# Attention and two gated feed-forward blocks on one core: x summed in HBM by accumulating transfers, PSUM emptied by ScalarE, the last tokens written in place

## The chip, the cores and the metric

The kernel runs on one core of a Trainium2 chip: TensorE (PE in the rows), VectorE (DVE), ScalarE (ACT), GpSimd (POOL) and SyncE (SP), which here issues the transfers. The metric is the device time of one execution in microseconds, and lower is better.

## The reference

```python
# attention: B=8, H=8, S=576, D=64
q_s = softmax(q, over d); k_s = softmax(k, over s)
x = q_s @ (k_s^T @ v)                     # heads side by side: (8, 576, 512)
# first block
h = gelu_tanh(x @ w_in)                   # 512 -> 1024
u, v = halves of h
v_n = (v - mean) / sqrt(var + 1e-6) * g_ln
v_s = w_sg @ v_n + b_sg                   # over the 576 tokens
x = x + (u * v_s) @ w_out                 # 512 -> 512
# second block
h = relu(x @ w_in2)                       # 512 -> 1024
c = conv over tokens, width 3, one filter per channel
out = (h * sigmoid(c)) @ w_out2           # 1024 -> 512
```

All data are float32.

## The kernel before, in words

**Numbers.** TensorE reads float32r. A float32 operand is therefore split into a high part (rounded to float32r) and a low part (the rest), and a product is made of three matmuls: high by high, high by low, low by high. In the rows a trailing h or l names the part (gh, gl; yh, yl; xh, xl).

**The plan.** The program is first written down and then put in order. A class `Plan` records each instruction as a `Node` with its engine, its reads and writes; `price` gives each a cost and a latency by hand-set numbers, `deadlines` works backward from the end, and `order` is a list scheduler that puts out one queue per engine. All recorded instructions go out through one line, L403, so the line of a row tells nothing and the tiles' names do. Each engine works through its queue in order.

**Part one (to about 570 us).** For each of the 8 batches b the attention makes `x_hi[b]` and `x_lo[b]` (128 partitions x 4 chunks x 576 tokens). Softmax's scaling of q and k is done partly on GpSimd (`q<-q,qm`, `kt<-kt,scr`). Then the first block runs in 29 groups per batch, over two halves of 288 tokens. Of a half, `hv` and `hu` make v and u (gelu on ScalarE), `mx` applies w_sg, gl and gh are the parts of u times v_s, and `wo` multiplies by w_out into four PSUM tiles `acc`. When the fourth chunk is in (dc == 3), VectorE evacuates the four tiles, adding x_hi, into `x2s` (one buffer), and SyncE stores it to `x2d[b]` in HBM. x_lo goes to HBM by itself, as `xld[b]` (for batch 0 GpSimd adds it to x2s instead). While this runs, `split_far` splits the second block's weights into parts and stores them in HBM; the pieces in work are called wsl.

**Part two (from about 570 us).** Batches 0 and 1 are multiplied directly (`h2`). Batches 2 to 7 use seven products of half-size blocks in place of eight; GpSimd forms the sums of weights (`weight_sums`, tiles tk and tn) and of x (`operands`, tiles xf and xg). `load_x` loads x2d[b] as xf; `add_low` loads xld[b] in four pieces xg and GpSimd adds them. Per 128 channels the convolution runs on VectorE (a product and two three-operand steps `cv<-h,cw,cv`), ScalarE makes the sigmoid, and `gate` makes yh and yl, 576 tokens wide, for the product with w_out2 (`o2`, tiles wAh and wAl hold the weights). A batch's 576 tokens are four groups of 128 and one of 64. The last 64 tokens of an even batch and its odd neighbour are put side by side in `yL` by GpSimd (two casts per gate) and multiplied together (`o2_pair`).

Of the kernel before, what the change touches and what calls it, by code (L numbers as in the profile page):

```python
# [11 lines left out]
F32 = mybir.dt.float32  # L12
# [7 lines left out]
DM = H * D  # L20
# [4 lines left out]
MODES_ = 'dppddpddppdpdppdpdpddddp'  # L25
CFG = {'dord': 'qqkqqkqwkkwwv', 'start': 'kaaatabbktbkbqkTawtqbqtQvwwvxxqxswxlwLc', 'gh': 'aaa', 'x2': 'nnn', 'hvl': [6, 5, 3], 'qs': 'ppppd', 'qm': 'pppdp', 'vb': 2, 'gb': 2, 'kt': 'dddd', 'sgl': 'dppp', 'rh': 'pd', 'sw': 'ada', 'sl': 'ada', 'gl': 'ddd'}
GUARD = 1.125 * 2.0 ** -15

# [104 lines left out]
class Node:  # L133
    __slots__ = ("eng", "name", "args", "kw", "cost", "lat", "deps", "succ", "late", "unit", "shared", "table", "kb", "i", "left", "ready", "done", "t", "hook")

# [9 lines left out]
class Plan:  # L145
# [3 lines left out]
    def __init__(self, real):  # L149
        self.real, self.nodes, self.unit = real, [], 0  # L150
        for k in real:
            setattr(self, k, Engine(self, k))

    def begin(self):
        self.unit += 1

    def node(self, eng, name="", args=(), kw={}):
        n = Node()
        n.eng, n.name, n.args, n.kw, n.i, n.unit = eng, name, args, kw, len(self.nodes), self.unit
        n.deps, n.succ, n.table, n.kb, n.shared, n.cost, n.lat, n.hook = {}, [], None, 0, False, 0.0, 0.0, None  # L160
        self.nodes.append(n)
        return n

# [17 lines left out]
    def touch(self, n, v, write):  # L181
        b = v.tile
        if b.prev is not None:
            for m in b.prev.nodes:
                n.deps[m.i] = "start" if m.eng == n.eng != "sp" else "end"
        g = b.pool.gate
        if g is not None:
            n.deps[g.i] = "start"
        p, c = v.region()
        keep = []  # L190
        for e in b.log:
            m, ep, ec, ew = e
            if m is n:
                keep.append(e)
                continue
            hit = (ep & p) and (ec & c)
            if hit and (write or ew):
                n.deps[m.i] = "start" if m.eng == n.eng != "sp" else n.deps.get(m.i, "end")
            if not (write and (ep & ~p) == 0 and (ec & ~c) == 0):
                keep.append(e)  # L200
        keep.append((n, p, c, write))
        b.log = keep
        b.nodes.append(n)

    def price(self, n, out, ins):
# [18 lines left out]
        elif e == "act":  # L224
            n.cost = 0.15 + cols * 0.00091
            n.lat = n.cost + 0.12
            f = args_func(n)
            n.table = {"Gelu_apprx_tanh": "g", "Exp": "e", "Sigmoid": "s"}.get(f)
        elif e == "pool":
            if "tensor" in name:  # L230
                n.cost = 0.8 if cols == 1 else 0.2 + cols * (0.0008 if name == "tensor_copy" else 0.00195)
            else:
                n.cost = 0.05 + cols * 0.0009
            n.lat = n.cost + 0.1
            n.shared = True
        else:
            two = sum(v.tile.space != "psum" for v in ins) > 1 and not psum and name in ("tensor_tensor", "scalar_tensor_tensor")
            fast = not psum and name in ("tensor_scalar", "tensor_copy") and out.tile.dtype == F32
            n.cost = 0.07 + cols * (0.0066 if name == "reciprocal" else 0.00058 if fast else 0.00117)
            n.lat = n.cost + 0.07  # L240
            n.shared = (two or fast) and cols > 60

    def deadlines(self):
# [7 lines left out]
        for n in self.nodes:  # L251
            for d in n.deps:
                self.nodes[d].succ.append(n)
        for n in reversed(self.nodes):
            for s in n.succ:
                c = n.lat if s.deps[n.i] == "end" else 0.0
                n.late = min(n.late, s.late - c)

    def order(self):
# [41 lines left out]
        def start(n, t):  # L301
# [6 lines left out]
            if n.eng == "pool":  # L308
                if vecend[0] > t:
                    more = min(cost, vecend[0] - t) * 0.3  # L310
                    cost, lat = cost + more, lat + more
                poolend[0] = t + cost
# [99 lines left out]
def attn_gated_conv_kernel(ctx, tc, q, k, v, q0, k0, w_in, g_ln, w_sgT, b_sg, w_out, w_in2, conv_w, w_out2, out):  # L412
# [25 lines left out]
    x2d = [dram.tile([128, KC, S], F32, name=f"x2d{b}") for b in range(B)]  # L438
    xld = [dram.tile([128, KC, S], F32, name=f"xld{b}") for b in range(B)]
    w2d = [dram.tile([128, KC, FF2], F32, name=f"w2d{n}") for n in "hl"]  # L440
# [282 lines left out]
    def xt(b, hp):  # L723
# [101 lines left out]
    def wo(b, j):  # L825
# [160 lines left out]
    xt_left(0)  # L986
    xt_copy(0)
    def w_job(i):
        split(slots[ORDER[i]], *jobs[i], None)
# [52 lines left out]

    def split_far(src, d, k, n, behind):
        for c in range(k):
            for f in range(0, n, NW):
                fs = slice(f, f + NW)
                slot, h = parts[njob[0] % 2]
                njob[0] += 1
                split(slot, src[:, c, fs], far_h, slot[1].bitcast(F32R), NW, (pool, pool), [t[:, c, fs] for t in d], behind)

# [97 lines left out]
    for b in range(B):  # L1148
# [13 lines left out]
        for i, g in enumerate(groups):  # L1162
# [16 lines left out]
    wo2_hi, wo2_lo = w2["ohi"], w2["olo"]  # L1179
    yL = [p2.tile([128, NFC, 128], F32R, name=f"yL{n}") for n in "hl"]  # L1180
    later = []
    h_t = [w2["pool"].tile([128, S + 2], F32, name=f"h{i}") for i in range(3)]
# [36 lines left out]
    def gate(b, fc, h, cv):  # L1219
        yh = p2.tile([128, S], F32R, tag="yh", bufs=4)  # L1220
        yl = p2.tile([128, S], F32R, tag="yl", bufs=4)
        act.activation(cv, cv, AF.Sigmoid)
        dve.tensor_tensor(cv, cv, h[:, 1:S + 1], ALU.mult)
        act.activation(yh, cv, AF.Copy)
        dve.tensor_tensor(yl, cv, r32(yh), ALU.subtract)
        o = 64 * (b % 2)
        yL_hi, yL_lo = yL
        def copies():
# [3 lines left out]
        if any(o_[0] < b and b % 2 == 0 for o_ in oq):  # L1232
            later.append(copies)
        else:
            copies()
        y_t[b, fc] = (yh, yl)
# [24 lines left out]
    def o2_pair(b, fcs):  # L1261
# [4 lines left out]
        for fc in fcs:  # L1266
            mm3(lp["t"], yL_hi[:, fc], yL_lo[:, fc], wo2_hi[:, fc], wo2_lo[:, fc], fc == 0, fc == NFC - 1)
        if NFC - 1 in fcs:
# [10 lines left out]
    def do_o():  # L1279
        b_, fc_ = oq.pop(0)  # L1280
        o2(b_, fc_)
        if seen[b_] == NFC and b_ % 2 == 1 and b_ < B - 1:
            o2_pair(b_, range(NFC))
            while later:
                later.pop(0)()

    FIRST = 2
# [52 lines left out]
    def operands(b, xf):  # L1340
        q = {"11": xf[:, 0:2, 0:HALF], "12": xf[:, 2:4, 0:HALF], "21": xf[:, 0:2, HALF:S], "22": xf[:, 2:4, HALF:S]}
        s1 = p2.tile([128, S], F32, tag="xg", bufs=3).rearrange("p (c t) -> p c t", c=2)
        mine = opn[b] = {}
# [87 lines left out]
    for b in range(FIRST):  # L1431
        for fc in range(NFC):
# [10 lines left out]
            if b == 0 and fc >= 4:  # L1443
                add_low(1, xf, fc - 4)
# [84 lines left out]
```

## Time and profile before

| what | value |
|---|---|
| median of 3 runs | 981.03 us |
| lowest and highest | 979.24 and 983.11 us |
| profiled execution | 981.86 us |
| its span | 980.1 us |
| its mean granted TensorE clock | 0.988 |
| last matmul's end to the end of the span | about 7.3 us |

The span is what the profile's rows cover; the profiled execution is 1.8 us longer than it. A granted clock of 1.00 is TensorE's full speed. The busy time of an engine leaves out the issuing of transfers and waiting on semaphores.

### The profile page before, as it was taken

The page shows a single profiled execution, that of the slowest core. Times are in us where ns is not written, and L with a number is a line of the kernel's source. Part 1 is how long each engine was busy: PE and PEld are TensorE (multiplying, and loading weights), DVE is VectorE, ACT ScalarE, POOL GpSimd, SP SyncE. Part 2 cuts the span into 40 slices and gives each one's busy share as a digit, 9 for nine tenths or more (in the row PEclk, how much of TensorE's full clock was granted, in tenths as well). Part 3 has the DMA queues.
Part 4 walks back from the last instruction along what each step waited for, and adds up shares of the span by engine and source line. Part 5 has one row for each costly group of instructions (what it writes and reads, how often), then busy time and mean ns, then how long its engine had stood idle before and what let it go on. Part 6 is the DMA issues. An engine that isn't in the chain of part 4 may idle for free.

```text
span 980.1 us, 16191 instructions
## 1 busy us (share of the span) xinstructions
PE 934.7 (95%) x6026; PEld 825.9 (84%) x6026; DVE 784.5 (80%) x1391; ACT 556.9 (57%) x1063; POOL 458.2 (47%) x500
## 2 busy tenths in 40 slices
PE   5989989998999999999999998999999999999996
PEld 4567778987989889899999997888998889888985
DVE  6988989799788897976867379997888878887773
ACT  6878356845666458453634244444766566656662
POOL 5326363556353754554434079644354626362110
PEclk9999989999999999999999999999999999999999
DMA  9451534250352625534256631313121313121001
GB/s 294 139 171 66 148 121 133 104 170 17 127 175 91 178 65 167 148 108 141 85 191 202 226 133 45 107 35 106 46 96 45 106 46 105 36 82 33 18 27 54
DMA packets 55590, 107.42 MB, mean 110 GB/s; under 512 B 5716, under 2 KB 29268, under 8 KB 52824
## 3 DMA queue, kind: packets, MB, share of 16 engines
q1 hardware_dynamic: 55512, 106.39, 34.5%
q8 instruction: 47, 0.77, 0.3%
q14 instruction: 31, 0.25, 0.1%
HBM read 70.85 MB, written 35.53 MB: 109 GB/s over the span
## 4 chain that ended last, share of the span: by engine, by line
PE 60%; DVE 11%; POOL 3%; issue 3%; ACT 2%; DMA 1%; SPq 0%; DVEq 0%; ACTq 0%; POOLq 0%
PE mm L403 39%; PE acc L403 21%; DVE cv L403 4%; POOL tk L403 1%; DVE yl L403 1%; POOL xf L403 1%; DMA out<-ot 1%; DVE xl L403 1%; DVE wsl L403 1%; DVE scr L403 1%; DVE lt L403 0%; DVE h L403 0%; DVE gl L403 0%; ACT cv L403 0%; DVE ot L403 0%
## 5 line engine op out<-in xcount | busy, mean ns | idle before, releaser
L403 DVE SCALAR_TENSOR_TENSOR cv<-h,cw,cv 128x576 f32<-128x576 f32 x128 | 132.3, 1034 | 27.8 <-ACT cv L403 25.7
L403 POOL CAST yLh<-yh 128x64 fp32r<-128x64 f32 x64 | 38.6, 603 | 152.6 <-ACT yh L403 152.6
L403 PE MATMUL acc<-wAh,yl 128*128 128x512 f32 x256 | 102.8, 402 | 6.6 <-DVE yl L403 6.6
L403 PE MATMUL acc<-wAh,yh 128*128 128x512 f32 x256 | 102.8, 402 | 0.3 <-ACT yh L403 0.2
L403 PE MATMUL acc<-wAl,yh 128*128 128x512 f32 x256 | 102.3, 400 | 0.0
L403 PE MATMUL acc<-gl,wouth 128*128 128x288 f32 x256 | 78.5, 307 | 4.8 <-DVE gl L403 4.8
L403 PE MATMUL mm<-xh,w2h 128*128 128x288 f32 x280 | 82.6, 295 | 0.4 <-ACT ot L403 0.4
L403 PE MATMUL acc<-gh,wouth 128*128 128x288 f32 x256 | 82.9, 324 | 0.0
L403 PE MATMUL mm<-xl,w2h 128*128 128x288 f32 x280 | 82.5, 295 | 0.0
L403 PE MATMUL mm<-xh,w2l 128*128 128x288 f32 x280 | 82.3, 294 | 0.0
L403 PE MATMUL mm<-sgh,vnh 128*128 128x288 f32 x256 | 80.8, 315 | 0.0
L403 PE MATMUL mm<-xh,wAh 128*128 128x288 f32 x256 | 80.5, 315 | 0.1
L403 POOL TENSOR_TENSOR wsl<-wsl 128x256 f32<-128x256 f32 (+2 forms) x66 | 50.1, 761 | 59.8 <-ACT wsl L403 18.6
L403 PE MATMUL acc<-gh,woutl 128*128 128x288 f32 x256 | 77.9, 304 | 0.0
L403 PE MATMUL mm<-xh,wAl 128*128 128x288 f32 x256 | 75.7, 296 | 1.4 <-ACT wAl L403 1.4
L403 PE MATMUL mm<-sgh,vnl 128*128 128x288 f32 x256 | 75.5, 295 | 0.0
L403 PE MATMUL mm<-sgl,vnh 128*128 128x288 f32 x256 | 75.5, 295 | 0.0
L403 PE MATMUL mm<-xl,wAh 128*128 128x288 f32 x256 | 75.5, 295 | 0.0
L403 ACT ACTIVATE cv<-cv 128x576 f32<-128x576 f32 x64 | 43.7, 683 | 54.9 <-DVE cv L403 54.6
L403 POOL TENSOR_TENSOR q<-q,qm 128x512 f32<-128x512 f32 x56 | 61.6, 1129 | 20.5 <-DVE qm L403 13.4
L403 DVE TENSOR_TENSOR cv<-cv,h 128x576 f32<-128x576 f32 x64 | 59.2, 926 | 14.3 <-ACT cv L403 13.5
L403 PEld LDWEIGHTS acc<-wAh,yl 128*128 128x128 f32 x256 | 48.9, 191 | 20.7 <-DVE yl L403 8.8
(276 smaller groups left out, 3028.9 us busy)
## 6 DMA issues: line engine op xcount, KB each, us to landing
vt<-in_v SPq DMA_DIRECT2D x8, 1152.0 KB, 10.2
x2d<-x2s SPq DMA_DIRECT2D x16, 576.0 KB, 3.8
out<-ot SPq DMA_DIRECT2D x32, 256.0 KB, 2.0
kt<-in_k SPq DMA_DIRECT2D x7, 1152.0 KB, 5.7
xld<-xl SPq DMA_DIRECT2D x7, 1152.0 KB, 5.3
xf<-x2d SPq DMA_DIRECT2D x7, 1152.0 KB, 5.1
xg<-xld SPq DMA_DIRECT2D x28, 288.0 KB, 2.8
q<-in_q SPq DMA_DIRECT2D x28, 256.0 KB, 2.7
```

The lines of the kernel that those rows point to most:

```text
L403: getattr(self.real[n.eng], n.name)(*[val(a) for a in n.args], **{k: val(v) for k, v in n.kw.items()})
```

## The change

The change has four parts.

1. **x in HBM.** A new function `x_out(b)` stores x_hi to x2d[b] (SyncE) and then adds x_lo to it by a transfer that accumulates, issued by GpSimd. Each half of the w_out product is added to x2d in the same way. So xld, its loads as xg and GpSimd's adds of them are gone.
2. **Evacuation.** ScalarE copies the four acc tiles to x2s; VectorE did it before.
3. **Last tokens.** yh and yl are 512 tokens wide; ScalarE and VectorE write the last 64 straight into yL, which becomes a ring of 11 slots. GpSimd's casts and the list `later` are gone.
4. **The plan's numbers.** `price` has other costs for ScalarE, GpSimd and VectorE; a transfer issued by GpSimd costs 1.2 us and lands after 20. Of `split_far`'s 32 pieces one goes in per some four groups, by `soon` and FAR, where all were recorded at once; the weight sums are recorded at (0, 6) and (1, 2) and may not start before the matmul recorded last.

The number of transfers that GpSimd issues goes from 0 to 24 (8 of x_lo, 16 of x2s). SyncE loses 28 loads of xg, 7 stores to xld and 16 of x2s, and has 8 stores of x_hi more. The program of after has 29 table loads on ScalarE, that of before 45.

```diff
@@ price
         elif e == "act":
-            n.cost = 0.15 + cols * 0.00091
-            n.lat = n.cost + 0.12
+            n.cost = (0.155 if psum else 0.195) + cols * 0.00085
...
         elif e == "pool":
+            if "dma" in name:
+                n.cost, n.lat = 1.2, 20.0
+                return
...
@@ xt
-                sp.dma_start(xld[b], r32(x_lo[b]))
+                x_out(b)
...
+    def x_out(b):
+        sp.dma_start(x2d[b], r32(x_hi[b]))
+        pool.dma_start(x2d[b], r32(x_lo[b]), accum_op=ALU.add, max_dma_last_dim=2304)
@@ wo
             for m in range(4):
-                if CFG['x2'][min(b, 2)] == 'a':
-                    act.activation(x2s[:, m], acc["t"][m][:, 0:HALF], AF.Copy)
-                    pool.tensor_tensor(x2s[:, m], x2s[:, m], r32(x_hi[b][:, m, cs]), ALU.add)
-                else:
-                    dve.tensor_tensor(x2s[:, m], acc["t"][m][:, 0:HALF], r32(x_hi[b][:, m, cs]), ALU.add)
-                if b == 0:
-                    pool.tensor_tensor(x2s[:, m], x2s[:, m], r32(x_lo[b][:, m, cs]), ALU.add)
-            sp.dma_start(x2d[b][:, :, cs], x2s)
+                act.activation(x2s[:, m], acc["t"][m][:, 0:HALF], AF.Copy)
+            pool.dma_start(x2d[b][:, :, cs], x2s, accum_op=ALU.add)
...
-            if b == 1 and i == 0:
-                mark = next(n for n in reversed(plan.nodes) if n.eng == "pe")
-                split_far(w_in2_v, w2d, KC, FF2, mark)
-                split_far(w_out2_v, wo2d, NFC, DM, mark)
+            if far and 29 * b + i >= 37 + 140 * (32 - len(far)) / 32:
+                plan.soon(FAR, split_far)
...
@@ gate
-        yh = p2.tile([128, S], F32R, tag="yh", bufs=4)
-        yl = p2.tile([128, S], F32R, tag="yl", bufs=4)
+        yh = p2.tile([128, 512], F32R, tag="yh", bufs=YB)
+        yl = p2.tile([128, 512], F32R, tag="yl", bufs=YB)
         act.activation(cv, cv, AF.Sigmoid)
         dve.tensor_tensor(cv, cv, h[:, 1:S + 1], ALU.mult)
-        act.activation(yh, cv, AF.Copy)
-        dve.tensor_tensor(yl, cv, r32(yh), ALU.subtract)
...
-            pool.tensor_copy(yL_hi[:, fc, o:o + 64], r32(yh[:, 512:576]))
-            pool.tensor_copy(yL_lo[:, fc, o:o + 64], r32(yl[:, 512:576]))
...
+        act.activation(yh, cv[:, 0:512], AF.Copy)
+        dve.tensor_tensor(yl, cv[:, 0:512], r32(yh), ALU.subtract)
...
+        zh, zl = (t[:, sl, 64 * (b % 2):64 * (b % 2) + 64] for t in yL)
+        act.activation(zh, cv[:, 512:S], AF.Copy)
+        dve.tensor_tensor(zl, cv[:, 512:S], r32(zh), ALU.subtract)
...
-    def add_low(b, xf, c):
-        xg = p2.tile([128, S], F32, tag="xg", bufs=3)
-        sp.dma_start(xg, xld[b][:, c])
-        pool.tensor_tensor(xf[:, c], xf[:, c], xg, ALU.add)
...
@@ weight_sums
+        after = plan.last
...
-            pool.tensor_tensor(t, r32(wq[n][0][:, c]), r32(wq[n][1][:, c]), ALU.add)
+            pool.tensor_tensor(t, r32(wq[n][0][:, c]), r32(wq[n][1][:, c]), ALU.add).deps[after.i] = "start"
@@ operands, first()
-            for c in range(4):
-                add_low(b, xf, c)
             pool.tensor_tensor(s1, q["21"], q["22"], ALU.add)
@@ main loop of part two
-            if b == 1 and fc in (0, 2):
-                weight_sums(fc // 2)
+            if (b, fc) in SUMS:
+                weight_sums(SUMS.index((b, fc)))
```

**The order on GpSimd in part two.** Here one batch's operands begin, in the kernel before; xg holds a piece of the low part until it is the sum s1, and the numbers behind the names tell tiles apart.

```order
L403 TENSOR_TENSOR xf_5671<-xf_5671,xg_5721 128x576
L403 CAST yLh_5814<-yh_5964 128x64
L403 TENSOR_TENSOR xf_5671<-xf_5671,xg_5676 128x576
L403 CAST yLl_5842<-yl_5976 128x64
L403 TENSOR_TENSOR xf_5671<-xf_5671,xg_5715 128x576
L403 TENSOR_TENSOR xf_5671<-xf_5671,xg_5721 128x576
L403 TENSOR_TENSOR xg_5715<-xf_5671 128x576
L403 TENSOR_TENSOR xf_5671<-xf_5671 128x2x288
```

The four adds of the low part stand ahead of the batch's first sum, with casts of the gates between. The queue of after at one of the same places:

```order
L424 TENSOR_TENSOR xg_6043<-xf_5720 128x576
L424 TENSOR_TENSOR xf_5720<-xf_5720 128x2x288
L424 TENSOR_TENSOR xf_5720<-xg_6043,xf_5720 128x2x288
```

Only the sums of x are left there.

**The evacuation.** In the kernel before it stands in VectorE's queue; the words in brackets name the semaphores that an instruction waits for (DMAHW those of SyncE's transfers).

```order
L403 TENSOR_TENSOR xLl_100<-mm_138,xLh_97 128x4x64 [waits Activation_49]
L403 TENSOR_TENSOR x2s_131<-acc_0_205,xh_0_994 128x288 [waits DMAHW1_49,PE_49]
L403 TENSOR_TENSOR x2s_131<-acc_0_210,xh_0_994 128x288 [waits PE_49]
L403 TENSOR_TENSOR x2s_131<-acc_0_217,xh_0_994 128x288 [waits PE_49]
L403 TENSOR_TENSOR x2s_131<-acc_0_226,xh_0_994 128x288 [waits PE_49]
L403 STREAM_TRANSPOSE q_0_239<-q_0_239 128x512 [waits Pool_49]
```

After, it stands in ScalarE's queue, behind a gelu of v, and waits for a transfer that GpSimd issued (DMASW).

```order
L424 ACT_TABLE_LOAD
L424 ACTIVATE v_434<-mm_172 128x512 [waits PE_49]
L424 ACTIVATE x2s_130<-acc_0_205 128x288 [waits DMASW7_49]
L424 ACTIVATE x2s_130<-acc_0_210 128x288
L424 ACTIVATE x2s_130<-acc_0_219 128x288
L424 ACTIVATE v_411<-mm_181 128x512 [waits PE_49]
L424 ACTIVATE x2s_130<-acc_0_227 128x288
```

The work has moved to another engine, and what stands around it is the next batch's gelu in place of the attention's transposes.

**GpSimd in part one, after.** Where only the scaling of q and the splitting of weights stood, transfers now stand between; the second one here is of x_lo.

```order
L424 TENSOR_TENSOR q_0_212<-q_0_212,qm_721 128x512 [waits DMAHW3_49,DVE_49]
L424 DMA x2d_0_1614<-x2s_130 512x1x288 [waits DMASW5_49,Activation_49]
L424 TENSOR_TENSOR q_0_221<-q_0_221,qm_721 128x512 [waits DMAHW7_49]
...
L424 DMA x2d_0_2367<-xl_0_1044 128x4x576 [waits DMAHW5_49]
```

The transfer of a half waits for ScalarE and for an earlier accumulating transfer, and the next scaling of q stands behind it.

## Rows read from the trace of the kernel before

**Rows 1.** The profile's page: each engine's busy time, share of the span, instructions
```profile
PE 934.7 (95%) x6026; PEld 825.9 (84%) x6026; DVE 784.5 (80%) x1391; ACT 556.9 (57%) x1063; POOL 458.2 (47%) x500
```

**Rows 2.** Stretches: start:end, length, busy PE, PEld, DVE, ACT, POOL, clock, DMA, GB/s
```profile
20.00:100.00 80.00, 76.64 (x452) 54.04 (x452) 69.40 (x136) 64.05 (x123) 32.48 (x32) 1.00 0.44 136
100.00:240.00 140.00, 130.51 (x914) 116.34 (x913) 123.83 (x271) 79.00 (x147) 73.64 (x77) 0.95 0.41 121
...
560.00:640.00 80.00, 73.08 (x448) 65.75 (x447) 68.93 (x70) 33.41 (x62) 61.42 (x50) 0.98 0.32 107
720.00:740.00 20.00, 17.86 (x108) 16.08 (x107) 17.53 (x21) 11.69 (x23) 15.45 (x13) 1.00 0.28 90
820.00:840.00 20.00, 18.22 (x104) 16.21 (x103) 18.39 (x21) 12.80 (x26) 15.40 (x13) 0.92 0.33 103
```

**Rows 3.** The same view in steps of 10 us
```profile
120.00:130.00 10.00, 8.33 (x59) 7.62 (x57) 9.59 (x21) 1.49 (x3) 6.04 (x6) 1.00 0.70 225
130.00:140.00 10.00, 8.95 (x39) 8.06 (x41) 7.39 (x20) 6.18 (x7) 8.36 (x10) 0.66 0.17 59
```

**Rows 4.** TensorE's waits, 20 to 560 us: total, times, longest
```profile
PE acc L403 <- DVE gl L403: 4.0, 3, 2.7
```

**Rows 5.** TensorE's waits, 560 to 960 us
```profile
PE acc L403 <- DVE yl L403: 5.9, 4, 2.5
PE mm L403 <- DVE h L403: 3.9, 2, 2.1
```

**Rows 6.** VectorE's groups, 580 to 640 us: busy us, mean ns | idle before
```profile
L403 DVE SCALAR_TENSOR_TENSOR cv<-h,cw,cv 128x576 f32<-128x576 f32 x19 | 28.0, 1474 | 0.4
L403 DVE TENSOR_TENSOR cv<-cv,h 128x576 f32<-128x576 f32 x10 | 11.6, 1162 | 1.2 <-ACT cv L403 1.1
```

**Rows 7.** VectorE's groups, 920 to 960 us
```profile
L403 DVE SCALAR_TENSOR_TENSOR cv<-h,cw,cv 128x576 f32<-128x576 f32 x15 | 12.2, 821 | 6.8 <-ACT cv L403 6.5
...
L403 DVE TENSOR_TENSOR cv<-cv,h 128x576 f32<-128x576 f32 x7 | 5.2, 755 | 2.3 <-ACT cv L403 2.3
```

**Rows 8.** GpSimd's groups over the whole span
```profile
L403 POOL TENSOR_TENSOR xf<-xf,xg 128x576 f32<-128x576 f32 x28 | 46.0, 1656 | 2.6 <-DMA xf<-x2d 2.6
...
L403 POOL CAST yLh<-yh 128x64 fp32r<-128x64 f32 x64 | 38.6, 603 | 152.6 <-ACT yh L403 152.6
```

**Rows 9.** GpSimd's groups, 580 to 640 us
```profile
L403 POOL TENSOR_TENSOR xf<-xf,xg 128x576 f32<-128x576 f32 x8 | 14.1, 1767 | 0.0
...
L403 POOL CAST yLh<-yh 128x64 fp32r<-128x64 f32 x9 | 6.3, 696 | 8.1 <-ACT yh L403 8.1
L403 POOL CAST yLl<-yl 128x64 fp32r<-128x64 f32 x9 | 5.5, 610 | 2.2 <-DVE yl L403 2.2
```

**Rows 10.** Groups of ScalarE and VectorE over the whole span
```profile
L403 ACT ACT_TABLE_LOAD x45 | 57.7, 1283 | 3.1 <-PE mm L403 1.7 <-PEq L1519 0.7
...
L403 ACT ACTIVATE tk<-mm 128x288 f32<-128x288 f32 x72 | 28.4, 399 | 6.9 <-PE mm L403 6.8
...
L403 DVE TENSOR_TENSOR x2s<-acc,xh 128x288 f32<-128x288 f32 x64 | 26.2, 451 | 5.1 <-PE acc L403 3.6 <-DMA wsl<-in_w_out 1.5
```

**Rows 11.** Tile x2s: issues, ns min/median/max, first and last start
```profile
L403 SPq DMA_DIRECT2D x2d<-x2s x16: 524/560/2640, 119.3 to 570.4; - x16
```

**Rows 12.** The page's DMA issues: KB each, median us from issue to landing
```profile
vt<-in_v SPq DMA_DIRECT2D x8, 1152.0 KB, 10.2
x2d<-x2s SPq DMA_DIRECT2D x16, 576.0 KB, 3.8
```

**Rows 13.** Timeline of SyncE's queue: start, length, both in us
```profile
188.44 0.53 SPq L403 DMA_DIRECT2D x2d<-x2s  x1
...
556.32 0.56 SPq L403 DMA_DIRECT2D x2d<-x2s  x1
```

**Rows 14.** Timeline of VectorE at the next evacuations
```profile
207.32 1.54 DVE L403 TENSOR_TENSOR x2s<-acc,xh 128x288 f32<-128x288 f32 x4
...
568.69 1.66 DVE L403 TENSOR_TENSOR x2s<-acc,xh 128x288 f32<-128x288 f32 x4 [0.62 <-PE acc L403]
```

More of the change, by code (lines that the diff above doesn't have):

```diff
@@ L133 @@
 class Node:
-    __slots__ = ("eng", "name", "args", "kw", "cost", "lat", "deps", "succ", "late", "unit", "shared", "table", "kb", "i", "left", "ready", "done", "t", "hook")
+    __slots__ = ("eng", "name", "args", "kw", "cost", "lat", "deps", "succ", "late", "unit", "shared", "table", "kb", "i", "left", "ready", "done", "t", "hook", "due")
 class Engine:
@@ L149, in __init__, with soon @@
     def __init__(self, real):
-        self.real, self.nodes, self.unit = real, [], 0
+        self.real, self.nodes, self.unit, self.due, self.last = real, [], 0, None, None
         for k in real:
             setattr(self, k, Engine(self, k))
+    def soon(self, lead, job):
+        self.due = (self.last, lead)
+        job()
+        self.due = None
     def begin(self):
@@ L159, in node @@
         n.eng, n.name, n.args, n.kw, n.i, n.unit = eng, name, args, kw, len(self.nodes), self.unit
-        n.deps, n.succ, n.table, n.kb, n.shared, n.cost, n.lat, n.hook = {}, [], None, 0, False, 0.0, 0.0, None
+        n.deps, n.succ, n.table, n.kb, n.shared, n.cost, n.lat, n.hook, n.due = {}, [], None, 0, False, 0.0, 0.0, None, self.due
         self.nodes.append(n)
+        if eng == "pe":
+            self.last = n
         return n
@@ L184, in touch @@
             for m in b.prev.nodes:
-                n.deps[m.i] = "start" if m.eng == n.eng != "sp" else "end"
+                n.deps[m.i] = "start" if m.eng == n.eng and "dma" not in m.name else "end"
         g = b.pool.gate
@@ L197, in touch @@
             if hit and (write or ew):
-                n.deps[m.i] = "start" if m.eng == n.eng != "sp" else n.deps.get(m.i, "end")
+                n.deps[m.i] = "start" if m.eng == n.eng and "dma" not in m.name else n.deps.get(m.i, "end")
             if not (write and (ep & ~p) == 0 and (ec & ~c) == 0):
@@ L229, in price @@
         elif e == "pool":
+            if "dma" in name:
+                n.cost, n.lat = 1.2, 20.0
+                return
             if "tensor" in name:
-                n.cost = 0.8 if cols == 1 else 0.2 + cols * (0.0008 if name == "tensor_copy" else 0.00195)
+                wide = any(o[0] == "to_broadcast" for v in views for o in v.ops)
+                n.cost = 0.95 if cols == 1 else 0.2 + cols * (0.0008 if name == "tensor_copy" else 0.00164 if wide else 0.0021)
             else:
@@ L238, in price @@
             fast = not psum and name in ("tensor_scalar", "tensor_copy") and out.tile.dtype == F32
-            n.cost = 0.07 + cols * (0.0066 if name == "reciprocal" else 0.00058 if fast else 0.00117)
+            n.cost = 0.15 + cols * (0.0062 if name == "reciprocal" else 0.00055 if fast else 0.00104)
+            if len(ins) > 2 or (fast and len(ins) > 1):
+                n.cost += min(cols, 500) * 0.00013
             n.lat = n.cost + 0.07
@@ L254, in deadlines @@
         for n in reversed(self.nodes):
+            if n.due:
+                n.late = n.due[0].late + n.due[1]
             for s in n.succ:
@@ L309, in start @@
                 if vecend[0] > t:
-                    more = min(cost, vecend[0] - t) * 0.3
+                    more = min(0.5, vecend[0] - t)
                     cost, lat = cost + more, lat + more
@@ L987, in attn_gated_conv_kernel @@
     xt_copy(0)
+    x_out(0)
     def w_job(i):
@@ L1041, in attn_gated_conv_kernel, with split_far @@
     njob = [0]
[L1043 to L1049, printed above, removed]
+    far = []
+    for src, d, kc, n in ((w_in2_v, w2d, KC, FF2), (w_out2_v, wo2d, NFC, DM)):
+        far += [(src, d, c, slice(f, f + NW)) for c in range(kc) for f in range(0, n, NW)]
+    def split_far():
+        src, d, c, fs = far.pop(0)
+        slot, h = parts[njob[0] % 2]
+        njob[0] += 1
+        split(slot, src[:, c, fs], far_h, slot[1].bitcast(F32R), NW, (pool, pool), [t[:, c, fs] for t in d], plan.last)
     far_h = p1.tile([128, NW], F32R, name="farh")
@@ L1179, in attn_gated_conv_kernel, with last_slot @@
     wo2_hi, wo2_lo = w2["ohi"], w2["olo"]
-    yL = [p2.tile([128, NFC, 128], F32R, name=f"yL{n}") for n in "hl"]
-    later = []
+    NL = NFC + 3
+    yL = [p2.tile([128, NL, 128], F32R, name=f"yL{n}") for n in "hl"]
+    held = {}
+    def last_slot(b, fc):
+        turn_ = fc if b < FIRST else 2 * (fc % 4) + (fc < 4)
+        return (b // 2 * NFC + turn_) % NL
     h_t = [w2["pool"].tile([128, S + 2], F32, name=f"h{i}") for i in range(3)]
@@ L1219, in gate @@
     def gate(b, fc, h, cv):
-        yh = p2.tile([128, S], F32R, tag="yh", bufs=4)
-        yl = p2.tile([128, S], F32R, tag="yl", bufs=4)
+        yh = p2.tile([128, 512], F32R, tag="yh", bufs=YB)
+        yl = p2.tile([128, 512], F32R, tag="yl", bufs=YB)
         act.activation(cv, cv, AF.Sigmoid)
         dve.tensor_tensor(cv, cv, h[:, 1:S + 1], ALU.mult)
-        act.activation(yh, cv, AF.Copy)
-        dve.tensor_tensor(yl, cv, r32(yh), ALU.subtract)
-        o = 64 * (b % 2)
-        yL_hi, yL_lo = yL
-        def copies():
-            pool.tensor_copy(yL_hi[:, fc, o:o + 64], r32(yh[:, 512:576]))
-            pool.tensor_copy(yL_lo[:, fc, o:o + 64], r32(yl[:, 512:576]))
[L1232 to L1235, printed above, removed]
+        act.activation(yh, cv[:, 0:512], AF.Copy)
+        dve.tensor_tensor(yl, cv[:, 0:512], r32(yh), ALU.subtract)
+        sl = last_slot(b, fc)
+        assert held.get(sl, (b // 2, fc)) == (b // 2, fc)
+        held[sl] = (b // 2, fc)
+        zh, zl = (t[:, sl, 64 * (b % 2):64 * (b % 2) + 64] for t in yL)
+        act.activation(zh, cv[:, 512:S], AF.Copy)
+        dve.tensor_tensor(zl, cv[:, 512:S], r32(zh), ALU.subtract)
         y_t[b, fc] = (yh, yl)
@@ L1283, in do_o @@
             o2_pair(b_, range(NFC))
-            while later:
-                later.pop(0)()
-    FIRST = 2
     xg2 = {}
```

15 lines of the change are left out of this document (11 added, 4 removed).

## The prediction

> **What bounds the kernel now.** I read the busy times first: TensorE is busy 934.7 us, 95% of the span [rows 1]. The change leaves all matmuls as they are, only in another order, so it can recover only what TensorE loses: idle time, and time at a lower granted clock. The table by stage says where that is [rows 2]. 20 to 100 us: 80 − 76.64 = 3.4 us idle. 100 to 240: 140 − 130.51 = 9.5 idle, at a granted clock of 0.95, which costs another 0.05 × 140 = 7.0. 560 to 640: 6.9 idle and 0.02 × 80 = 1.6 of clock. 720 to 740: 2.1 idle. 820 to 840: 1.8 idle and 0.08 × 20 = 1.6 of clock. The clock comes from the idle time: TensorE stands 1.7 us of the ten from 120, and in the ten from 130 the granted clock is 0.66 with TensorE busy 8.95 [rows 3]; part of that stretch ran at 1.2 instead of 2.4 GHz. Sum: 19.9 us in part one (3.4 + 9.5 + 7.0) and 14.0 in part two (8.5 + 2.1 + 3.4): 33.9 in all. I leave the first 20 us and the tail out, since their work stays.
>
> Next, for whom TensorE waits there. In part one its longest wait is for VectorE's gl, 4.0 us in three waits [rows 4]; in part two for VectorE's yl, 5.9 in four, and its h, 3.9 in two [rows 5]. VectorE is busy 123.83 of 140 us in the first of these stretches and 17.53 and 18.39 of 20 in the last two [rows 2]: it, not ScalarE (79.00 of 140) or GpSimd, is late. Why it is late in part two can be seen where the same instruction is held against itself: the convolution's three-operand step takes 1474 ns from 580 to 640, and the add of the gate 1162 [rows 6]; from 920 to 960, where GpSimd has little left to do, 821 and 755 [rows 7]. VectorE is slowed by work of GpSimd beside it.
>
> **The change, part by part.** *GpSimd's adds and casts go.* Over the whole run: 46.0 us of 28 adds of the low part of x, and 38.6 of 64 small casts [rows 8], beside 64 more of the same size. From 580 to 640 they are 14.1 + 6.3 + 5.5 = 25.9 us [rows 9], 42% of the 61.42 that GpSimd is busy from 560 to 640 [rows 2]; the sums of weights and operands stay. Were GpSimd silent there, VectorE would save 19 × (1474 − 821) + 10 × (1162 − 755) ns = 12.4 + 4.1 = 16.5 us. 42% of that is 7, about the 6.9 idle there. The two later stretches hold the same adds and casts, GpSimd busy 15.45 and 15.40 of 20 [rows 2].
>
> *The last 64 tokens* cost VectorE a subtract of 64 columns more per gate, against 64 columns less in the one before. No row has the small one: no more than the 451 ns of a 288-column evacuation [rows 10], no less than what the shorter one saves (64/576 of about 1 us, 0.1). For nine gates between 580 and 640 that is −0 to +3.2 us net; I take +1, nearer to the low end, since 64 columns are far fewer than 288. ScalarE gets a copy in the same manner, and is busy 33.41 of 80 there [rows 2]: hidden. So part two gives back 7 − 1 = 6 of 6.9 in its first stretch; with the clock and the two others in the same proportion, I take 12 of the 14.0.
>
> *The evacuation of the w_out product* goes from VectorE to ScalarE: VectorE loses 64 × 451 ns = 26.2 us, ScalarE gains about 64 × 399 = 25.5, by the row of its copies of 288 columns, and loses 16 of its 45 table loads of 1283 ns, 20.5 us [rows 10]. It stays under 60% busy, so this is hidden, unless ScalarE waits (below). 1.64 us of VectorE in each of 16 halves; 140 us hold four of them, 6.6 us, so VectorE would go from 123.83 to about 117 in the stretch where TensorE stands 9.5 us. But VectorE still has its bursts, and the rest of the attention's operations stay; no row says which burst is shortened. Bounds: nothing, or all 19.9. I take 4 of the 9.5, half of the clock (3.5), and 0.5 of the 3.4: 8.
>
> *The order* comes from new planner costs. What it gains or loses by itself can't be read from a row; outside the stretches of the sum I count no loss of TensorE, so a worse order can only lose there. I take 0, with ±6 us (a third of part one's 19.9) in the range.
>
> *24 accumulating transfers issued by GpSimd.* None is in the trace before. Issue: SyncE spends 560 ns in the median and 2640 at most on such a store [rows 11]; 24 of them make 13 to 63 us on GpSimd, which is idle 66 of the 140 us from 100 [rows 2], and is otherwise relieved by the adds and casts of part two. Behind them in GpSimd's queue stand the key and query products that attention needs; 0.56 to 2.64 us late each, hidden as long as GpSimd is ahead. But the issue of a half also waits, by its order, for ScalarE's evacuation and for the transfer that wrote the same rows of x2d before, and holds GpSimd's queue meanwhile; a queue held for as long as the landing, 10 us, would show in VectorE and TensorE. Landing: no shorter than the plain store of these 576 KB, 3.8 us; I take twice a 1152 KB load, 2 × 10.2 = 20 us, as the upper bound, since an accumulation reads and writes [rows 12]. Middle: 10. What waits for it: x2s has one buffer, so the next half's evacuation, now on ScalarE, waits for the landing, and v's and u's gelus stand behind it in ScalarE's queue. Once in a batch that window is narrow: the stores of a half at 188.4 and 556.3 us [rows 13] are followed by the next evacuation at 207.3 and 568.7 [rows 14], 18.9 and 12.4 us later. The new order puts the evacuation behind one more gelu of v, so a landing of 12 to 20 us fits in. At 10 nothing waits.
>
> The Trainium skill speaks against this part: by "SBUF — State Buffer", section "SBUF: two separate sides", a transfer issued from GpSimd has its descriptors written by GpSimd's cores, and while VectorE runs in a mode that takes both of its ports, GpSimd is locked out and the descriptors starve. No run here yet shows an issue from GpSimd; that VectorE and GpSimd hold each other up is what [rows 6, 7] show. By that rule the transfers would be late just where VectorE is busiest, which is the fourth rival.
>
> *Loads.* 28 reloads of low parts and 7 stores of them go from SyncE, and 8 stores of x come; nothing in TensorE's waits is for a transfer there, so 0.
>
> **The sum.** The profiled execution spans 980.1 us and took 981.86; the median of the runs is 981.03. 981.86 − 8 − 12 = 961.9, and 0.8 less by the median: **961 us**.
>
> **The rivals.**
> 1. *Forecast* (chance 0.55): both parts give some, 953 to 970.
> 2. *Everything goes* (0.10): VectorE has enough slack that no stall and no dip of the clock is left: 981 − 33.9 = 947. For it: VectorE is the only one waited for at length. Against it: it is still busy over 80% from 100 to 240 then, and a burst needs no average.
> 3. *Only part two* (0.13): the new order and GpSimd's issues cost part one what VectorE gains there: 981 − 12 = 969 or so, up to 974. For it: part one's waits are short and for several tiles, so no one of them is removed by name.
> 4. *The wait changes its place* (slower, 0.12): the accumulation lands later than the window, some 18 us. From there each of the 8 batches loses the excess once in ScalarE's queue, with gelus and then matmuls behind it. At 27 us of landing that is 8 × 9 = 72 us, less the 20 gained: about 1030; at 22 us, 8 × 4 − 20 = 12: 993. For it: one buffer, and a queue in which the wait blocks everything behind it. Against it: 576 KB land in 3.8 us when stored plainly.
> 5. *No change* (0.10): GpSimd's adds did not slow VectorE, but the weight sums did, which stay, or GpSimd's 24 issues of 2 to 3 us each give back what is gained: 976 to 986. For it: from 580 to 640, 58% of GpSimd's work remains.
>
> **The numbers.** I hold a change of less than 0.5% (4.9 us) for no change that a measurement of this kernel could tell. Faster: rivals 1 to 3, 0.55 + 0.10 + 0.13 = 0.78. Same: 0.10. Slower: 0.12. The range takes in "everything goes" at its lower end and reaches into "no change" at its upper: 946 to 979; outside lie the slower case and half of the fifth.
>
> **What would show it.** Right: from 560 to 640, idle time of TensorE falls from 6.9 to 2 us or less, and the three-operand step takes nearer 1200 than 1474 ns; the granted clock of 100 to 240 rises above 0.95; VectorE is busy some 7 us less there. Wrong: ScalarE waits for the queue of GpSimd's transfers ahead of x2s with TensorE waiting for v or u behind it (rival 4), GpSimd's issues stand before key or query products for which TensorE waits (rivals 3 and 5), or the three-operand step keeps its 1474 ns with the adds gone (rival 5). The forecast falls as a whole if TensorE's idle time from 20 to 240 us grows above the 12.9 (3.4 + 9.5) that it is now.

## The result, and the profile after

The changed kernel takes 966.18 us in the median of 4 runs (965.54 to 969.03), the kernel before 981.26 in the same comparison (979.24 to 983.11, 4 runs): a ratio of 0.9852, 95% interval 0.9825 to 0.988. The forecast was 961, between 946 and 979. The profiled execution took 965.54 us, 3.6 more than the 961.9 that the sum gave for it.

The same stretches as in [rows 2], of after (columns as there):

```profile
20.00:100.00 80.00, 77.32 (x475) 55.20 (x474) 65.66 (x131) 61.16 (x118) 34.63 (x32) 1.00 0.57 168
100.00:240.00 140.00, 132.50 (x936) 118.71 (x935) 119.09 (x254) 74.23 (x153) 70.61 (x71) 0.98 0.56 136
...
560.00:640.00 80.00, 76.30 (x469) 69.41 (x469) 63.12 (x82) 36.47 (x80) 30.15 (x21) 0.98 0.19 58
...
720.00:740.00 20.00, 20.00 (x122) 18.11 (x121) 17.33 (x31) 14.82 (x33) 1.45 (x1) 1.00 0.14 54
...
820.00:840.00 20.00, 20.00 (x121) 18.08 (x120) 15.87 (x27) 13.46 (x28) 1.44 (x1) 1.00 0.08 32
```

From 720 to 740 and from 820 to 840 TensorE no longer stands, and the granted clock of the second is 1.00 in place of 0.92. From 560 to 640 it stands 3.7 us in place of 6.9, at the same 0.98. From 100 to 240 it stands 7.5 in place of 9.5, at 0.98 in place of 0.95. The DMA engines are busier from 20 to 240 (0.57 and 0.56 in place of 0.44 and 0.41). Of the signs that the prediction set, the granted clock and the three-operand step (below) came; the idle time from 560 to 640 stayed above the 2 us named, and VectorE lost 4.7 us from 100 to 240 in place of some 7.

TensorE's waits of after, 20 to 560 us and behind the dots 560 to 960, as in [rows 4, 5]:

```profile
PE mm L424 <- DVE kvd L424: 5.1, 3, 3.7
...
PE acc L424 <- DVE gl L424: 0.8, 2, 0.5
...
PE acc L424 <- DVE yl L424: 3.4, 2, 2.0
```

The wait for gl has shrunk from 4.0 to 0.8, that for h is gone, and a wait for kvd is now the longest in part one. VectorE's groups from 580 to 640 us, as in [rows 6]:

```profile
L424 DVE SCALAR_TENSOR_TENSOR cv<-h,cw,cv 128x576 f32<-128x576 f32 x20 | 19.4, 972 | 0.4
L424 DVE TENSOR_TENSOR cv<-cv,h 128x576 f32<-128x576 f32 x11 | 12.3, 1118 | 2.0 <-ACT cv L424 2.0
L424 DVE TENSOR_TENSOR yl<-cv,yh 128x512 fp32r<-128x512 f32 x11 | 10.5, 955 | 2.2 <-ACT yh L424 2.1
...
L424 DVE TENSOR_TENSOR yLl<-cv,yLh 128x64 fp32r<-128x64 f32 x11 | 5.7, 516 | 0.0
```

The three-operand step takes 972 ns in place of 1474. The new subtract of 64 columns takes 516 in the mean, though it has an eighth of the columns of yl's (955). Its row from 920 to 956 us, where GpSimd does nothing in this trace:

```profile
L424 DVE TENSOR_TENSOR yLl<-cv,yLh 128x64 fp32r<-128x64 f32 x7 | 1.5, 220 | 0.3 <-ACT yLh L424 0.3
```

The 516 is a mean of two lengths. Of the 64 small subtracts in the whole trace, 55 take 210 to 225 ns. The other 9 take 1309 to 1471; each of them starts while GpSimd is at a tensor-tensor instruction and ends some 80 ns behind that one's end. One of them, from the timelines of GpSimd and of VectorE (start, length in us):

```profile
607.45 1.80 POOL L424 TENSOR_TENSOR tn0l<-tk,tn0h 128x512 fp32r<-128x512 f32 x1
608.03 1.31 DVE L424 TENSOR_TENSOR yLl<-cv,yLh 128x64 fp32r<-128x64 f32 x1
```

The three-operand steps of the kernel before tell GpSimd's two kinds of work apart. Counted in the records of its trace, 59 of the 128 overlap nothing on GpSimd by more than 0.1 us and take 817 ns in the mean, 34 overlap casts alone and take 813, and 35 overlap a tensor-tensor instruction and take 1614. So it is the adds and sums on GpSimd that hold VectorE up here, and not the casts. In the changed kernel 13 of the 128 overlap a tensor-tensor instruction.

The accumulating transfers, first the page's DMA issues (KB each, us to landing), with SyncE's plain store of x_hi:

```profile
x2d<-xh SPq DMA_DIRECT2D x8, 1152.0 KB, 5.0
x2d<-xl POOLq DMA_DIRECT2D x8, 1152.0 KB, 13.1
x2d<-x2s POOLq DMA_DIRECT2D x16, 576.0 KB, 6.9
```

and the rows of tile x2s (ns min/median/max):

```profile
L424 ACT ACTIVATE x2s<-acc x64: 391/412/454, 108.4 to 571.1; 128x288 f32<-128x288 f32 x64
...
L424 POOL DMA_DIRECT2D x2d<-x2s x16: 1204/1231/1242, 110.4 to 572.0; - x16
```

An accumulation of a half lands in 6.9 us where the plain store of [rows 12] took 3.8, that of x_lo in 13.1 where the plain store of x_hi, as large, takes 5.0. Issuing one of a half takes GpSimd 1.2 us. The next evacuation follows no sooner than 19.6 us behind an issue in this trace, so ScalarE never waits for a landing: its waits ahead of x2s are for TensorE alone.

Where the longest wait for kvd comes from, 3.7 of the 5.1 us, shows in the chain of after between 188 and 201 us (start, length, what):

```profile
188.19 9.16 DMA wsl<-in_w_in
...
197.44 0.10 ACT wsl L424
...
198.42 0.44 ACT gh L424
...
199.97 0.28 DVE kvd L424
200.27 0.30 DVE kvd L424
...
200.62 0.43 PE mm L424 x2
```

and in GpSimd's timeline just before it:

```profile
183.03 1.24 POOL L424 DMA_DIRECT2D x2d<-x2s  x1 [1.49 <-ACT x2s L424]
183.74 1.85 POOL L424 DMA_DIRECT2D x2d<-xl  x1
```

The load of a far weight piece, wsl, is issued at 188.19 and takes 9.16 us, while the accumulation of x_lo issued at 183.74 is in flight (it lands at 197.7). ScalarE waits for the piece; the making of gh stands behind it in ScalarE's queue; VectorE waits for gh, with kvd behind it; TensorE waits for kvd. Over the whole of part one (140 to 570 us), the far pieces' loads and stores, counted one by one in the records of the traces:

```
              no accumulation in flight    one in flight
kernel        count  mean us  max us       count  mean us  max us
before           70     3.13     5.7           0
after            24     2.47     5.1          46     4.81     9.3
```

The longer time beside an accumulation shows in each of the six kinds of far transfer by itself. It is not the mark of an accumulation alone: in two kernels below that have none, e1 and e4, a far store of 128 KB took 9.6 and 8.4 us at the longest, each issued 0.7 us behind a 1152 KB load of v.

### The profile page after: what moved, and what is told of

Its sections match the earlier page's. It is cut to its first block, busy times and chain, and to the rows that moved or that the text cites. A ratio compares the mean times of both kernels' runs of the same rounds, so it can differ in the third digit from the quotient of the medians.

```text
span 963.8 us, 16047 instructions
## 1 busy us (share of the span) xinstructions
PE 927.9 (96%) x6026; PEld 822.1 (85%) x6026; DVE 751.7 (78%) x1391; ACT 558.5 (58%) x1175; POOL 361.4 (37%) x360
## 4 chain that ended last, share of the span: by engine, by line
PE 79%; DVE 12%; DMA 4%; ACT 3%; issue 2%; SPq 0%; POOL 0%; ACTq 0%; DVEq 0%
PE mm L424 53%; PE acc L424 25%; DMA wsl<-in_w_in 1%; DVE cv L424 1%; DVE qm L424 1%; DMA kt<-in_k 1%; DVE wsl L424 1%; DVE scr L424 1%; DVE xl L424 1%; ACT L424 1%; DVE gl L424 1%; DMA w2dh<-farh 1%; DVE vnl L424 1%; DVE lx L424 1%; DMA sgh<-in_q 1%
## 5 line engine op out<-in xcount | busy, mean ns | idle before, releaser
L424 DVE SCALAR_TENSOR_TENSOR cv<-h,cw,cv 128x576 f32<-128x576 f32 x128 | 113.5, 888 | 22.2 <-ACT cv L424 20.6
L424 POOL TENSOR_TENSOR q<-q,qm 128x512 f32<-128x512 f32 x56 | 63.9, 1202 | 28.9 <-DVE qm L424 12.9
L424 DVE TENSOR_TENSOR cv<-cv,h 128x576 f32<-128x576 f32 x64 | 56.9, 892 | 15.2 <-ACT cv L424 14.9
L424 POOL TENSOR_TENSOR kt<-kt,scr 128x512 f32<-128x512 f32 (+1 forms) x42 | 48.9, 1191 | 50.8 <-PE mm L424 37.2
L424 POOL TENSOR_TENSOR wsl<-wsl 128x256 f32<-128x256 f32 (+1 forms) x66 | 51.1, 775 | 43.5 <-DVE wsl L424 15.6
## 6 DMA issues: line engine op xcount, KB each, us to landing
x2d<-xl POOLq DMA_DIRECT2D x8, 1152.0 KB, 13.1
```

Source lines behind the costliest of these rows:

```text
L424: getattr(self.real[n.eng], n.name)(*[val(a) for a in n.args], **{k: val(v) for k, v in n.kw.items()})
```

## The experiments

Theory A, that of the prediction: the gain is work taken from GpSimd (part two) and from VectorE (part one). Rival P: the gain is the new order (the plan). After the first four runs a third was formed, theory C: accumulating transfers make the far pieces late, and the new order bears that better than the old.

For every kernel, TensorE's loss in part one (20 to 560 us) and in part two (560 to 840 us) was worked out as in the prediction, idle time plus (1 − granted clock) × length, from the stretches 20:100, 100:240, 240:400, 400:560, 560:640, 640:720, 720:740, 740:820, 820:840; the last but one column is what TensorE waited for kvd in part one, by the table of waits. Each loss is of one profiled execution, and the clock is read to two places, which can move a loss by about 1 us.

| kernel | median us | ratio to before, 95% | loss 1 | loss 2 | kvd us | what it has of the change |
|---|---|---|---|---|---|---|
| before | 981 | | 21.8 | 14.2 | 3.2 | nothing |
| after | 966.2 | 0.9852 (0.9825–0.988) | 15.8 | 5.4 | 5.1 | all |
| e1 | 977.7 | 0.9982 (0.9964–1.0001) | 20.0 | 7.4 | 1.0 | plan without VectorE's costs |
| e2 | 998.3 | 1.0193 (1.0166–1.022) | 33.7 | 16.5 | 10.6 | x, tokens |
| e3 | 967.4 | 0.9868 (0.9836–0.99) | 18.2 | 1.8 | 4.5 | plan, x |
| e4 | 967.4 | 0.9879 (0.9849–0.9909) | 10.0 | 10.0 | 0.3 | plan, tokens |
| e5 | 992.6 | 1.0111 (1.0075–1.0147) | 36.9 | 12.1 | 10.9 | x |
| e6 | 980.2 | 1.0002 (0.998–1.0025) | 17.7 | 15.1 | 3.2 | tokens |
| e7 | 996.6 | 1.0162 (1.0126–1.0198) | 41.6 | 7.2 | 15.6 | all but the costs |
| e8 | 976.8 | 0.9962 (0.9942–0.9982) | 20.8 | 12.0 | 8.2 | all but the spread |
| e9 | 960.0 | 0.9796 (0.9772–0.982) | 11.0 | 5.3 | 0.4 | all, far pieces later |
| e10 | 964.2 | 0.9842 (0.982–0.9864) | 13.4 | 2.1 | 0.7 | plan, tokens, 8 accumulations |
| e11 | 986.0 | 1.0055 (1.0037–1.0072) | 31.0 | 8.7 | 5.0 | e7 without x_lo |
| e12 | 965.1 | 0.9852 (0.981–0.9894) | 19.6 | 1.6 | none | e9 and e10 |

In e2, e5, e7 and e11 part one lasts 18 to 28 us longer (the last evacuation starts at 588 to 598 us, not at 570), so that the column of part two holds its end.

**e1, the plan alone, but for VectorE's costs.** On the kernel before, the new costs of ScalarE and GpSimd, `soon` and the spread of `split_far`, SUMS; nothing else. VectorE's costs, which the changed kernel has too, stay the old ones here, so that e1 is not the whole plan of which its expectation speaks.

```diff
-            if b == 1 and fc in (0, 2):
-                weight_sums(fc // 2)
+            if (b, fc) in SUMS:
+                weight_sums(SUMS.index((b, fc)))
```

> The kernel before with only the planner's new numbers (costs, spread of the far weight pieces, time of the weight sums); x by stores and reloads, evacuation on VectorE and GpSimd's adds and casts as before. Theory A, that the gain comes from work taken from GpSimd and VectorE: within 6 us of the time before, 975 to 987, and the three-operand step stays above 1300 ns from 580 to 640. Rival P, that the new order alone makes the gain: 971 or less.

977.71 us: theory A's range. The three-operand step keeps its length, since the adds beside it are still there:

```profile
L420 DVE SCALAR_TENSOR_TENSOR cv<-h,cw,cv 128x576 f32<-128x576 f32 x19 | 27.3, 1435 | 0.4
```

Yet the loss in part two fell from 14.2 to 7.4 with the same work. This much of the plan does little for the time, and it does do something for part two; what the whole plan does alone no run tells.

**e2, all but the plan.** The changed kernel with the old costs of ScalarE, GpSimd and VectorE (an accumulation keeps its price), with

```diff
-SUMS = ((0, 6), (1, 2))
+SUMS = ((1, 0), (1, 2))
...
-            if far and 29 * b + i >= 37 + 140 * (32 - len(far)) / 32:
-                plan.soon(FAR, split_far)
+            if b == 1 and i == 0:
+                mark = plan.last
+                while far:
+                    split_far(mark)
```

and without the weight sums' bound.

> The changed kernel with the planner's old costs, the far pieces recorded at once and the weight sums at (1, 0) and (1, 2); the work itself is that of the changed kernel. Theory A: the gain stays, 962 to 972. Rival P: it goes, 977 or more.

998.25 us: theory A falls as a sole cause, since the work without the plan is slower than the kernel before. P stands: it expected 977 or more, and e1, which gained nothing clear, lacks a part of the plan. Its chain ahead of a wait for kvd:

```profile
317.30 2.50 POOL x2d L419 x2
319.79 1.33 POOL wsl L419 x2
...
322.36 8.18 DMA w2dl<-wsl
...
331.56 0.29 DVE kvd L419
```

Two accumulations are issued at 317.3, the store of a far piece at 322.4 takes 8.18 us, and VectorE holds its queue for the piece's slot, with kvd behind. This is where theory C comes from.

**e3 and e4, one part of the work undone.** e3 gives the casts back to GpSimd:

```diff
-        act.activation(zh, cv[:, 512:S], AF.Copy)
-        dve.tensor_tensor(zl, cv[:, 512:S], r32(zh), ALU.subtract)
+        pool.tensor_copy(zh, r32(yh[:, 512:576]))
+        pool.tensor_copy(zl, r32(yl[:, 512:576]))
```

> The changed kernel with yh and yl 576 wide again and GpSimd's 128 casts into the ring of slots, in place of the copy on ScalarE and the subtract on VectorE. Theory A: GpSimd has 11.8 of its 25.9 us of 580 to 640 again and slows VectorE; 3 to 5 us slower than the changed kernel, about 970. Rival T, that the small subtracts on VectorE (516 ns each from 580 to 640) cost as much as the casts did: within 2 us of the changed kernel.

e4 gives x back its stores, reloads and adds, and VectorE its evacuation:

```diff
-                act.activation(x2s[:, m], acc["t"][m][:, 0:HALF], AF.Copy)
-            pool.dma_start(x2d[b][:, :, cs], x2s, accum_op=ALU.add)
+                dve.tensor_tensor(x2s[:, m], acc["t"][m][:, 0:HALF], r32(x_hi[b][:, m, cs]), ALU.add)
+            sp.dma_start(x2d[b][:, :, cs], x2s)
...
+            for c in range(4):
+                add_low(b, xf, c)
```

> The changed kernel with x as before: x_lo stored apart and reloaded, added by GpSimd, the w_out product evacuated by VectorE with x_hi added, no accumulating transfer. Theory A: VectorE has its 26 us of evacuations and GpSimd its 46 us of adds again; 7 us in part one and 4 to 6 in part two, 975 to 980. Rival P: within 3 us of the changed kernel, 963 to 969.

Both took 967.4. e3 bears out rival T: the casts cost no more than the subtracts, and TensorE has no idle time at all from 560 to 640 with the casts there, though the three-operand step takes 1225 ns in the mean from 580 to 640 (part one ends 5 us later here than in after):

```profile
560.00:640.00 80.00, 80.00 (x512) 74.09 (x511) 62.27 (x73) 36.25 (x71) 42.53 (x39) 1.00 0.26 74
```

e4 is out of theory A's range by 8 us, and within that of rival P. Its part one, with VectorE's 26 us of evacuations back, loses 10.0 us where after loses 15.8:

```profile
100.00:240.00 140.00, 134.39 (x997) 120.15 (x996) 127.71 (x281) 75.19 (x144) 71.95 (x75) 1.00 0.41 124
```

VectorE is busier there (127.71 against 119.09), and TensorE stands less (5.6 against 7.5) at full clock. Its part two, with the adds back, loses 10.0 where after loses 5.4, and the three-operand step takes 1191 ns where after's takes 972:

```profile
L424 DVE SCALAR_TENSOR_TENSOR cv<-h,cw,cv 128x576 f32<-128x576 f32 x18 | 21.4, 1191 | 0.3
```

**e5 and e6, one part of the work under the old plan** (the edits of e2 with those of e3, and with those of e4).

> Old planner and GpSimd's casts; of the change only x in HBM: stores of x_hi, accumulating transfers of x_lo and x2s, evacuation on ScalarE, no reload and no add. Theory X, that it is the accumulating transfers and the evacuation on ScalarE which the old order does not suit (the run with all work changed under the old planner took 998): 992 to 1002. Rival T, that the last tokens are what the old order does not suit: 970 to 980.

> Old planner and x as before; of the change only the last tokens written in place by ScalarE and VectorE, without GpSimd's casts. Theory X: 972 to 980, since GpSimd loses 74 us of casts and nothing in part one is touched. Rival T: 988 or more.

992.62 and 980.16: theory X, clearly. Under the old plan x in HBM, with its accumulations and ScalarE's evacuation, costs 1.1%, with 10.9 us of waits for kvd in place of 3.2; the last tokens change nothing that can be measured. e4 is e6 with the new plan and no other difference, and takes 967.4 in place of 980.2, 0.9879 of before in place of 1.0002: with x as before the plan is worth 12 us, where the whole change is worth 15. So P is borne out for most of the gain, with the last tokens as they are after; whether the plan needs them is not shown.

**e7 and e8, one part of the plan undone.** e7 has the old costs, among them

```diff
-            n.cost = (0.155 if psum else 0.195) + cols * 0.00085
+            n.cost = 0.15 + cols * 0.00091
...
-            n.cost = 0.15 + cols * (0.0062 if name == "reciprocal" else 0.00055 if fast else 0.00104)
+            n.cost = 0.07 + cols * (0.0066 if name == "reciprocal" else 0.00058 if fast else 0.00117)
```

and e8 the edit on `split_far` shown with e2.

> The changed kernel with the planner's old costs of ScalarE, GpSimd and VectorE; the spread of the far pieces and the weight sums as in the changed kernel. If the costs are what makes the new order fit: 980 or more. If the spread of the far pieces is: within 4 us of the changed kernel, 964 to 971.

> The changed kernel with the 32 far pieces recorded at once at b = 1, i = 0, and the new costs. If the costs are what makes the new order fit: within 4 us of the changed kernel, 964 to 971. If the spread is: 980 or more, with VectorE waiting for stores of far pieces.

996.63 and 976.82. The costs are worth 30 us to the changed kernel, the spread of the far pieces 10.6; e8 lies between its two expectations. Which of the costs does it was not taken apart. That e1 lacks VectorE's and gains little, while e4 has them and gains, points at those; no run changes them alone.

**e9, the far pieces planned later.** One edit in the scheduler; a transfer with a due time belongs to a far piece:

```diff
                 lat = wire[0] + 1.9 - t
+                if n.due:
+                    lat += 6.0
```

> The changed kernel, with one line more in the planner: a transfer of a far piece is taken to land 6 us later than by its size. Nothing else changes but the order that follows. Theory C, that the accumulating transfers make the far pieces' loads and stores land late (2.5 us alone, 4.8 on average and up to 9.3 beside an accumulation), and that VectorE and ScalarE hold their queues for them with kvd behind: the 5.1 us of waits for kvd fall to 2 or less, 960 to 964. Rival O, that kvd is late by the order alone: the waits for kvd stay at 4 or more, 964 to 970.

960.01 us, as theory C has it. The wait for kvd in part one of e9:

```profile
PE mm L426 <- DVE kvd L426: 0.4, 1, 0.4
```

The accumulations are all there, and the far pieces beside them still take 4.4 us on average (37 of them, counted as above) against 2.5 for 34 alone. What changed is that TensorE no longer waits behind them. That the pieces are late for the accumulations and not for other traffic, this run doesn't show. It is the fastest kernel of the study; its interval and that of the changed kernel (0.9825 to 0.988) don't overlap.

**e10, a third of the accumulations.** x2s is evacuated by VectorE and stored as in e4, without the reloads and adds, x_hi is no longer stored by itself, and

```diff
+            sp.dma_start(x2d[b][:, :, cs], x2s)
+            if h == 1:
+                pool.dma_start(x2d[b], r32(x_lo[b]), accum_op=ALU.add, max_dma_last_dim=2304)
```

> The changed kernel with VectorE's evacuation and plain stores of x2s as before, and one accumulating transfer per batch, of x_lo, behind the second half; GpSimd's adds in part two stay gone. Theory C: 16 of the 24 accumulations are gone, so the far pieces land sooner and the waits for kvd fall to 2 us or less; VectorE has the 26 us again, which cost nothing where x as before was tried: 958 to 964. The forecast's own step, that VectorE's 26 us of evacuations cost part one some 8 us: 970 to 976.

964.18 us, at the upper end of theory C's range: 8 far transfers meet an accumulation in place of 46 (those 8 take 8.0 us on average), and kvd is waited for 0.7 us. The evacuations on VectorE cost nothing that shows.

**e11, fewer accumulations under the old costs.** e7 without the transfer of x_lo, so that x lacks its low part:

```diff
-        pool.dma_start(x2d[b], r32(x_lo[b]), accum_op=ALU.add, max_dma_last_dim=2304)
```

> As the run with the old costs (996.6), without the 8 accumulating transfers of x_lo, so x lacks its low part from part one. Theory C: a third of the transfers and half of their bytes are gone; the 15.6 us of waits for kvd fall below 8, 980 to 990. Rival A, that the old costs place ScalarE's evacuations badly, whatever the transfers do: the waits stay above 12, 992 to 1000.

986.03 us, with 5.0 us of waits for kvd in place of 15.6, as theory C has it. It is still slower than the kernel before, with 16 accumulations left; theory C explains the 10 us between e7 and e11 and not what is left.

**e12, e9 and e10 together.**

> The late low part and the planner's later landing of far pieces together. Theory C: with one accumulation per batch only 8 far transfers still meet one, so the line has little left to mend: 960 to 964, no better than the late landing alone (960.0). If the two gains are of different waits, they add up: 955 to 958.

965.14 us, 1 us above theory C's range. The gains don't add up, as theory C has it; that it is 5 us slower than e9 was not expected. It waits for kvd no more, but for xl, u and lt, in another order.

## Why the prediction was right, and where it was not

**The total.** The time lies in the range, 5 us above the forecast. Part two gave back 14.2 − 5.4 = 8.8 us of the 12 that were taken, part one 21.8 − 15.8 = 6.0 of 8. That it did so was in the main luck. The work was to make the whole gain of 20 us. With the new plan, x in HBM (e4 to after) and the last tokens (e3 to after) are each worth 1 to 3 us, which the intervals don't tell from nothing; the order, taken at 0, is worth 12 with x as before (e6 to e4). Rival 4 didn't come about: an accumulation lands in 6.9 us by the median, between the bounds of 3.8 and 20 and under the 10 that I took, and the window was 19.6 us or more.

**Part two.** That GpSimd's adds slow VectorE there was right: with x in HBM the loss falls from 10.0 to 5.4 us (e4 to after). The three-operand step fell further than the 1200 ns or so named, to 972. Three terms were mis-sized. The casts: I counted their 11.8 of the 25.9 us on GpSimd as a load on VectorE, and beside casts alone the three-operand step keeps its length (813 ns against 817). The share was off as well, since the 25.9 us of 580 to 640 were set against GpSimd's 61.42 of 560 to 640; from 580 to 640 it was busy 47.81, of which the adds alone are 14.1. The subtract of the last 64 tokens: I took 1 us net for nine gates, with 451 ns as its upper bound; its mean is 516, beside 160 less for yl, 955 after and before

```profile
L403 DVE TENSOR_TENSOR yl<-cv,yh 128x576 fp32r<-128x576 f32 x9 | 10.0, 1115 | 0.4 <-ACT yh L403 0.3
```

so 11 gates cost 3.9 us. What made it long is 3 of the 11 that met a tensor-tensor instruction of GpSimd. So the casts' removal is worth nothing (e3, e6). And the plan, taken at 0, gave part two 14.2 − 7.4 = 6.8 where only a part of it was there (e1), and 15.1 − 10.0 = 5.1 whole (e6 to e4).

**Part one.** Here the step failed that said that TensorE stands because VectorE is late, and so gains from 26.2 us less of evacuations on it ("I take 4 of the 9.5, half of the clock (3.5), and 0.5 of the 3.4: 8"). With the evacuations back on VectorE part one loses less, not more (e4, e10). Both drop accumulations as well; but e9, which has the evacuations on ScalarE and hardly waits for kvd, loses no less than e4 (11.0 against 10.0), so what VectorE is spared doesn't show. What made part one shorter is the order: the kernel before and e4 do the same work in part one and lose 21.8 and 10.0 there, so that the order is worth not the 6 us of the range but 11.8 (7.7 from e6 to e4). What x in HBM does in part one is the contrary of what I held: it costs 5.8 us with the new plan (15.8 after against 10.0 in e4), and 15 with the old (36.9 in e5 against 21.8). Most of the 5.8 goes where the far pieces are planned later (11.0, e9), which points at the late pieces and at what stands behind them in the queues of ScalarE and VectorE; of the 15 the waits for kvd are 7.7 (10.9 against 3.2), and the rest isn't taken apart. "I take 0, with ±6 us" and "nothing in TensorE's waits is for a transfer there, so 0" are the two sentences that hid it: I looked at what SyncE's queue loses, and not at what is in flight with what GpSimd issues. That the total still came out is two errors of opposite sign.

**The rule of the Trainium skill** that spoke against the transfers, "SBUF — State Buffer", section "SBUF: two separate sides": a transfer issued from GpSimd starves while VectorE runs in a mode that takes both of its ports. The rows don't show it at the issue: the 16 issues of x2s took 1204 to 1242 ns, whatever VectorE did beside them. The delay that the runs do show falls on SyncE's plain transfers, which the rule does not speak of.

**What stays open.** Which of the new costs matters; what the whole plan gives with the casts and x as before, or x in HBM over e4 with the line of e9 in both; why e12 is slower than e9; and what two transfers in flight share, since the runs show only that the plain ones take about twice as long beside an accumulation, and in e1 and e4 as long behind a large plain load.

## What to carry to other kernels

When a change adds transfers, ask which other transfers will be in flight with them, and what is queued behind the instructions that wait for those: a late piece of background work costs nothing until something urgent stands behind it in an engine's queue. Where a planner sets the order, its latency of a transfer should be that of the loaded machine; one line that says so was worth 6 us here. Undo each part alone and all together: here each of two parts of the work could be undone for 1 to 3 us, because the plan made most of the gain, and under the old plan the work made the kernel slower. And make sure that the part left in is whole: e1 lacked one engine's costs, and read as the plan alone it would have hidden this.

## What the runs showed of the hardware

An accumulation of 576 KB into HBM took 6.9 us where the plain store took 3.8, and one of 1152 KB 13.1 where the plain store took 5.0. Plain loads and stores of a far piece took 2.5 us alone and 4.8 beside one, 9.3 at most. A subtract of 64 columns on VectorE took 218 ns in the mean, and 1309 to 1471 where it began during a tensor-tensor instruction of GpSimd: it ended some 80 ns behind that one. Casts on GpSimd did not lengthen VectorE's three-operand step (813 ns against 817), tensor-tensor instructions did (1614). VectorE's evacuation of 288 columns out of PSUM was not lengthened by them: 448 to 452 ns on average with and without in the kernel before.
